# Issue order of the attention stretch set by a list scheduler inside the kernel

## The chip, the cores and the metric

The kernel runs on one core of one Trainium2 chip. A core has five engines that each work through their own list of instructions in order and wait for each other by semaphores: TensorE (PE, matrix products), VectorE (DVE), ScalarE (ACT), GpSimd (POOL) and SyncE (SP), which here issues every DMA transfer. The metric is the device time of one execution in microseconds, smaller being better. What is changed is only the order in which each engine's list stands; no instruction is added, removed or given other operands.

## The reference

The program is an attention with a threshold, and then two gated layers over its output.

```python
q, k, v: (4 batches, 8 heads, 576 rows, 64 columns), float32; tau = 0.02
scores = (q @ k.T) / sqrt(64)
scores = where(scores >= max(scores, row) - tau, scores, -1e9)
attn   = exp(scores - max) ; attn /= sum(attn) + 1e-9
x = (attn @ v), heads side by side: 2304 tokens x 512
# layer 1
x = (sigmoid(x @ w_gate) * (x @ w_val)) @ w_out          # 512 -> 1536 -> 512
# layer 2
x = ((x @ w1) * (x @ w2)) @ w3 @ w_out2                   # 512 -> 1024 -> 1024 -> 512
```

All inputs of the two layers arrive in 64-bit form, and the products are done in split precision: an operand is a high and a low part, and three products (high-low, low-high, high-high) are summed.

## The kernel before

The program has one stretch that this change concerns, up to the line `cut = ...` of the new code, and a tail behind it.

**The attention stretch** runs 144 steps, numbered 0 to 143: 4 batches x 4 pairs of heads x 9 row blocks. A step goes through the engines like this:

- `s_mm` (PE): 4 or 6 products of 128x288 into one of two PSUM buffers `ps_s`, in turn by step. So step n+2 needs the buffer of step n.
- `s_max` (DVE, L360): the row maximum `nm`. `s_exp` (ACT, L366 and L367): the exponential `e` and the threshold `th`. `s_mask` (DVE, L375): masks `e`, reading `ps_s` for the last time; this frees the buffer.
- `s_hi`, `s_lo` (ACT L383; ACT L394 and POOL L397, or DVE L399): the high and low 16-bit parts `h16`, four buffers.
- `s_tr` (SP, L403): a transposing DMA of `h16` into `pt`, five buffers.
- `pv` (PE): 14 products (28 in the ninth step of a pair) of `pt` with the value tiles, into `u` or a part of `ps_s`.

For each pair there is preparation too: loads of q, k and v, their transposes on PE (`ps_t`), a chain of small DVE and ACT operations for the scale of v (`vm`, `vx`, `vp`, `vs`, then `vb` on ACT at L304), and at the pair's end `x_norm`, `x_pe`, `x_act`, which write the result into `XR`.

Two other pieces of work are traced between these steps by `filler`. The first is the **merge** (`merge_gen`): layer 2's `w3` and `w_out2` are loaded in pieces of 512 KB (SP, L477), turned from 64-bit into float (`cast64`: DVE L487 and L493, ACT L492, POOL L496), split (`wol`, DVE L506), transposed (`ps_3`, then `tl` at DVE L572) and multiplied into 8 tiles `ps_34` of 24 products. The second is **layer 1** (`l1_gen`) for the first three batches: cast of its weights, `ps_h` and `ps_o` products of 128x512, and the element-wise work on them. Layer 1 can start only when all four pairs of batch 0 are through, which is about step 41.

**The tail** finishes layer 1 for the last batch and does layer 2: `ps_h`, `ps_o`, `ps_ab` and `ps_y` products on PE.

What sets the order: the kernel is written in a tracing layer whose scheduler, when the program is finished, orders each engine's instructions by a priority (the place in the trace, and 90 places earlier for `s_mask`, `s_max`, `s_exp`, `s_mm`, by `tc.high_priority(offset=RING)`) and by its own simulation of when each could start. It then gives out the buffers and the semaphore waits. Once the program runs, the order on an engine is fixed: an instruction whose input is late holds everything behind it on that engine.

Of the kernel before, what the change touches and what calls it, by code (L numbers as in the profile page):

```python
# [16 lines left out]
ALU = mybir.AluOpType  # L17
AX = mybir.AxisListType
PSUM = bass.MemoryType.PSUM


@with_exitstack
def kernel(
# [22 lines left out]
    nc = tc.nc  # L46
    P = 128
    B, H, S, D = q.shape
# [16 lines left out]
    cst = ctx.enter_context(tc.tile_pool(name="cst", bufs=1))  # L65
    ps_m = ctx.enter_context(tc.tile_pool(name="ps_m", bufs=2, space=PSUM))
    ps_c = ctx.enter_context(tc.tile_pool(name="ps_c", bufs=1, space=PSUM))
    nbank = [0, (ps_m, ps_m)]
# [23 lines left out]
    ap_ = actx.enter_context(tc.tile_pool(name="attn", bufs=1, side="right"))  # L92
    ps_s = actx.enter_context(tc.tile_pool(name="ps_s", bufs=1, space=PSUM))
    ps_u = actx.enter_context(tc.tile_pool(name="ps_u", bufs=1, space=PSUM))

# [234 lines left out]
    def s_mm(g):  # L330
        pr, s = divmod(g, NSL)
        p = prep[pr]
        ps = sbuf_[g % 2][:, SO:SO + S]
        if s < 2 * NC:
            h, c = divmod(s, NC)
            cs = slice(c * P, (c + 1) * P)
            if pr < ZP:
                x, y = qst[h][pr % 2][:, cs], kst[h][pr % 2][:, cs]
                prods = [(x, p["xk"]), (y, p["xk"]), (x, p["yk"])]
            else:  # L340
                prods = [(p["qa"][h][:, cs], p["ka"][h]), (p["qa"][h][:, cs], ylz[h])]
        else:
            prods = [
                (p["qb"][:, 0, :], p["xk"]),
                (p["qb"][:, 1, :], p["xk"]),
                (p["qb"][:, 0, :], p["yk"]),
            ]
        for i, (a, r) in enumerate(prods):
            for j in range(2):
                mm(  # L350
                    ps[:, j * HS:(j + 1) * HS], a, r[:, j * HS:(j + 1) * HS],
                    i == 0, i == len(prods) - 1,
                )
        st[g] = {"ps": ps}

    def s_max(g):
        x = st[g]
        nm = ap_.tile([P, 1], F32, tag="nm", name="nm", bufs=3)
        th = ap_.tile([P, 1], F32, tag="th", name="th", bufs=3)
        nc.vector.tensor_reduce(nm, x["ps"], axis=AX.X, op=ALU.max, negate=True)  # L360
        x.update(nm=nm, th=th)

    def s_exp(g):
        x = st[g]
        e = ap_.tile([P, S], F32, tag="e", name="e", bufs=4)
        nc.scalar.activation(e, x["ps"], AF.Exp, bias=x["nm"])  # L366
        nc.scalar.activation(x["th"], x["nm"], AF.Identity, scale=-1.0, bias=ntau)  # L367
        x["e"] = e

    def s_mask(g):  # L370
        pr, s = divmod(g, NSL)
        x = st[g]
        if s == 0:
            prep[pr]["sum"] = ap_.tile([P, NSL], F32, tag="sum", name="sum", bufs=2)
        nc.vector.scalar_tensor_tensor(  # L375
            x["e"], x["ps"], x["th"], x["e"], op0=ALU.is_ge, op1=ALU.mult,
            accum_out=prep[pr]["sum"][:, s:s + 1],
        )

    def s_hi(g):  # L380
        x = st[g]
        x["h16"] = ap_.tile([P, 2 * S], F16, tag="h16", name="h16", bufs=4)
        nc.scalar.activation(  # L383
            x["h16"][:, 0:S], x["e"], AF.Copy, scale=PSC
        )

    def s_lo(g):
        e = st[g]["e"]
        hb = st[g]["h16"]
        hi, lo = hb[:, 0:S], hb[:, S:2 * S]  # L390
        b = g // (NPAIR * NSL)
        if b == 0 or g % 2 == 0:
            if b < 2:
                nc.scalar.activation(e, e, AF.Copy, scale=PSC)  # L394
            else:
                nc.gpsimd.tensor_scalar(e, e, PSC, 1.0, op0=ALU.mult, op1=ALU.mult)
            nc.gpsimd.tensor_tensor(lo, e, hi, op=ALU.subtract)  # L397
        else:
            nc.vector.scalar_tensor_tensor(lo, e, PSC, hi, op0=ALU.mult, op1=ALU.subtract)  # L399
# [24 lines left out]
    def x_norm(pr):  # L424
        p = prep[pr]
        rs = ap_.tile([P, NSL], F32, tag="rs", name="rs", bufs=1)
        nc.vector.tensor_scalar(rs, p["sum"], 1e-9, None, op0=ALU.add)
        nc.vector.reciprocal(rs, rs)
        xn = ap_.tile([P, NC, 2, D], F32, tag="xn", name="xn")
        xt = ap_.tile([P, 2, D], F32, tag="xt", name="xt")  # L430
        nc.vector.tensor_tensor(
            xn.rearrange("p c h d -> p h c d"), p["u"],
            rs[:, 0:2 * NC].rearrange("p (h c x) -> p h c x", h=2, x=1).to_broadcast([P, 2, NC, D]),
            op=ALU.mult,
        )
        nc.vector.tensor_scalar(
            xt, p["ut"][:, 0:P].rearrange("p (x d) -> p x d", x=2),
            rs[:, 2 * NC:NSL], None, op0=ALU.mult,
        )
        p.update(xn=xn, xt=xt)  # L440
# [82 lines left out]
    mp = None  # L523
# [91 lines left out]
    lp = None  # L615
    lx = None
    lb = None
# [6 lines left out]
    def open_lx():  # L624
        nonlocal lx
        lx = lx_ctx.enter_context(tc.tile_pool(name="lx", bufs=1))
# [193 lines left out]
    LAG = 5  # L820
# [4 lines left out]
    def run(gen, ns):  # L825
        while gen is not None and ns > 0:
            n = len(defer)
            t = next(gen, "end")
            if lp is None:
                flush(1)  # L830
            else:
                flush(max(len(defer) - n, 0))
            if t == "end":
                return None
            if t is None:
                return gen
            ns -= t
            spent[0] += t
        return gen
# [3 lines left out]
    def budget(g):  # L843


        n = NPAIR * NSL
        e = max(0, (g - LAG - 3) // n)
        return (e * L1_NS - spent[0]) / (2 * ((e + 1) * n + LAG + 3 - g)) if e else 1.0

    order = ExitStack()  # L850
# [5 lines left out]
    mp = mctx.enter_context(tc.tile_pool(name="mp", bufs=1))  # L856
# [22 lines left out]
    def filler(g, half):  # L879
        nonlocal l1, merge, lp, lb  # L880
        if merge is not None:
            merge = run(merge, 700.0)
            if merge is None:
                mctx.close()
                spent[0] = 0
                lp = tc_lp.enter_context(tc.tile_pool(name="lp", bufs=1))
                lb = tc_lp.enter_context(tc.tile_pool(name="lb", bufs=1))
                open_lx()
                l1 = l1_gen()
        elif l1 is not None and (g > NPAIR * NSL or g >= 10 and half):  # L890
            l1 = run(l1, budget(g))
# [14 lines left out]
    for g in range(G + LAG + 3):  # L906
        pr, s = divmod(g, NSL)
        steps = ahead[s] if pr + 1 < NP else ([],) * 5
        done = divmod(g - LAG, NSL)
        with tc.high_priority(offset=RING):  # L910
            if g < G:
                s_mask(g)
            if g + 1 < G:
                s_max(g + 1)
                s_exp(g + 1)
            if g + 2 < G:
                s_mm(g + 2)
        if g < G:
            s_hi(g)
        for f in steps[3]:  # L920
            f(pr + 1, g)
        if done[1] == 0 and done[0] > 0:
            x_norm(done[0] - 1)
        if g < G and g % 2 == 0 or g // (NPAIR * NSL) == 0:
            s_lo(g)
        if 0 < g <= G and not ((g - 1) % 2 == 0 or (g - 1) // (NPAIR * NSL) == 0):
            s_lo(g - 1)
        if 2 <= g < G + 2:
            s_tr(g - 2)
        for f in steps[0]:  # L930
            f(pr + 1)
        for f in steps[1]:
            f(pr + 1)
        if done[1] == 2 and done[0] > 0:
            x_act(done[0] - 1)
            if done[0] % NPAIR == 0:
                xdone[0] = done[0] // NPAIR
        filler(g, 0)
        for f in steps[2]:
            if isinstance(f, str):  # L940
                if pr + 2 < NP:
                    load(src[f], pr + 2, f)
            else:
                f(pr + 1)
        if 0 <= g - LAG < G:
            pv(g - LAG, g)
        for f in steps[4]:
            f(pr + 1)
        if done[1] == 1 and done[0] > 0:
            x_pe(done[0] - 1, g)  # L950
        filler(g, 1)
    order.close()
    actx.close()
    tail[0] = True
# [15 lines left out]

    ps_2 = ctx.enter_context(tc.tile_pool(name="ps_2", bufs=5, space=PSUM))
    nbank[1] = (ps_m, ps_m) + (ps_2,) * 5
# [86 lines left out]
    sp = ctx.enter_context(tc.tile_pool(name="sp", bufs=1))  # L1059
# [101 lines left out]
    for g in range(NG):  # L1161
# [22 lines left out]
        for t in range(GT // P):  # L1184
            part(NF2 - 2, t)
            part(NF2 - 1, t)
            out_rows(g, t, pss[t])

# [31 lines left out]
```

## Time and profile before

| | |
|---|---|
| median of 3 runs | 1117.62 us (1112.0 to 1119.1) |
| profiled execution | 1116.73 us, of which the span from first to last instruction is 1114.9 us |
| busy share of the span | PE 92%, weight loads 81%, DVE 72%, POOL 61%, ACT 56% |
| attention stretch | 0 to about 671 us |
| tail | about 671 to 1115 us |

The busy share is an average over stretches with different limits, so the table of stretches (the first group of rows below) is read before it: for each stretch of time it has the busy time of each engine. The waits then say, for one engine and one stretch, which instruction came late and by how much.

### The profile page before, as it was taken

The numbers are of one execution on the slowest core, as the hardware profiler recorded it, in microseconds if no ns is written. First come the engines' busy times: TensorE is split into PE (matmuls) and PEld (weight loads), VectorE is DVE, ScalarE is ACT, GpSimd is POOL, SyncE is SP. The second block draws the span as 40 slices with busy tenths as digits, with TensorE's granted clock in tenths as the row PEclk, the third lists the DMA queues.
The fourth block names the chain that finished last, engine by engine and source line by source line (L and its number), as shares of the span: only waits on it lengthen the run. The fifth ranks groups of instructions, "written<-read, shape, count | busy, mean of one in ns | idle before, by whom it ended". The sixth has DMA issues, their size and how long they took to land. (4 is left out here: it accounts for less than half of the span.)

```text
span 1114.9 us, 20240 instructions
## 1 busy us (share of the span) xinstructions
PE 1023.0 (92%) x7088; PEld 902.2 (81%) x7088; DVE 799.6 (72%) x1388; ACT 629.2 (56%) x1253; POOL 683.1 (61%) x585
## 2 busy tenths in 40 slices
PE   3599965899899999999999998999999999999997
PEld 2477764777778787787878888999999989988996
DVE  8998578899886887777887645776776644752741
ACT  4788787778586666677667645454442322331321
POOL 4655358488695676767687755775764633562430
PEclk8599986899899999999999999999999999999999
DMA  7799779899899898999999565676559826834922
GB/s 216 183 244 222 152 174 269 179 236 262 194 252 225 182 187 192 210 202 177 221 194 212 129 145 169 213 230 225 194 184 295 253 71 231 289 124 123 334 87 61
DMA packets 301845, 221.29 MB, mean 198 GB/s; under 512 B 221872, under 2 KB 250544, under 8 KB 301744
## 3 DMA queue, kind: packets, MB, share of 16 engines
q1 hardware_dynamic: 301744, 220.00, 76.7%
q8 instruction: 56, 0.92, 0.4%
q14 instruction: 45, 0.37, 0.1%
HBM read 133.17 MB, written 30.93 MB: 147 GB/s over the span
## 5 line engine op out<-in xcount | busy, mean ns | idle before, releaser
L366 ACT ACTIVATE e<-ps_s,nm 128x576 f32<-128x576 f32 x144 | 106.3, 739 | 73.2 <-DVE nm L360 72.2
L397 POOL TENSOR_TENSOR h<-e,h 128x576 f16<-128x576 f32 x90 | 120.0, 1334 | 40.3 <-ACT e L394 16.8
L63 PEld LDWEIGHTS <-pt 128*128 128x128 f16 x2240 | 83.8, 101 | 61.4 <-DMA pt<-h 29.7
L375 DVE SCALAR_TENSOR_TENSOR e<-ps_s,th,e 128x576 f32<-128x576 f32 x144 | 116.2, 811 | 19.9 <-ACT th L367 11.0
L360 DVE TENSOR_REDUCE nm<-ps_s 128x1 f32<-128x576 f32 x144 | 105.8, 748 | 29.5 <-PE ps_s L63 16.0
L383 ACT ACTIVATE h<-e 128x576 f16<-128x576 f32 x144 | 97.2, 678 | 37.1 <-DVE e L375 31.6
L63 PE MATMUL ps_h<-xl,vh 128*128 128x512 f32 (+1 forms) x240 | 92.8, 387 | 3.4 <-DVE yk L274 3.4
L63 PE MATMUL ps_h<-xl,gh 128*128 128x512 f32 (+1 forms) x240 | 92.2, 384 | 3.7 <-POOL xl L506 2.8
L63 PE MATMUL ps_y<-wm,abh 128*128 128x512 f32 x288 | 91.5, 390 | 1.2 <-DVE wm L506 1.2
L63 PE MATMUL ps_o<-gvl,oh 128*128 128x512 f32 (+1 forms) x240 | 91.0, 379 | 0.0
L506 POOL TENSOR_TENSOR gl<-w,gh 128x512 fp32r<-128x512 f32 x42 | 55.5, 1322 | 56.5 <-ACT gh L505 51.4
L63 PE MATMUL ps_h<-xh,vh 128*128 128x512 f32 (+1 forms) x240 | 89.9, 375 | 0.0
L63 PE MATMUL ps_h<-xh,vl 128*128 128x512 f32 (+1 forms) x240 | 89.8, 374 | 0.0
L63 PE MATMUL ps_h<-xh,gl 128*128 128x512 f32 (+1 forms) x240 | 88.9, 370 | 0.0
L63 PE MATMUL ps_h<-xh,gh 128*128 128x512 f32 (+1 forms) x240 | 88.8, 370 | 0.0
L63 PE MATMUL ps_o<-gvh,ol 128*128 128x512 f32 (+1 forms) x240 | 88.5, 369 | 0.0
L63 PE MATMUL ps_o<-gvh,oh 128*128 128x512 f32 (+1 forms) x240 | 88.5, 369 | 0.0
L63 PE MATMUL u<-vh,pt 128*128 128x64 f16 x640 | 64.5, 200 | 25.0 <-DMA pt<-h 21.9
L506 POOL TENSOR_TENSOR ol<-w,oh 128x512 fp32r<-128x512 f32 x42 | 54.0, 1294 | 30.3 <-ACT oh L505 30.2
L399 DVE SCALAR_TENSOR_TENSOR h<-e,h 128x576 f16<-128x576 f32 x54 | 67.8, 1256 | 5.4 <-ACT h L383 5.1
L506 POOL TENSOR_TENSOR vl<-w,vh 128x512 fp32r<-128x512 f32 x43 | 59.0, 1373 | 14.6 <-ACT vh L505 14.6
L506 POOL TENSOR_TENSOR gvl<-gr,gvh 128x512 fp32r<-128x512 f32 (+1 forms) x48 | 61.8, 1287 | 8.4 <-ACT gvh L505 7.9
(207 smaller groups left out, 3109.3 us busy)
## 6 DMA issues: line engine op xcount, KB each, us to landing
wc<-sc_c SPq DMA_DIRECT2D x168, 256.0 KB, 3.4
w<-sc_w SPq DMA_DIRECT2D x35, 768.0 KB, 5.2
sc_c<-wc SPq DMA_DIRECT2D x56, 256.0 KB, 2.5
XR<-in_moe_w_out_dram SPq DMA_DIRECT2D x20, 512.0 KB, 5.0
sc_w<-w SPq DMA_DIRECT2D x11, 768.0 KB, 5.6
XR<-in_moe_w_dram SPq DMA_DIRECT2D x16, 512.0 KB, 4.6
raw<-in_moe_w_dram SPq DMA_DIRECT2D x16, 512.0 KB, 4.5
XR<-in_moe_w_gate_dram SPq DMA_DIRECT2D x12, 512.0 KB, 5.4
```

What stands on the lines that cost most here:

```text
L63: nc.tensor.matmul(out_, lhsT, rhs, start=first, stop=last)
L360: nc.vector.tensor_reduce(nm, x["ps"], axis=AX.X, op=ALU.max, negate=True)
L366: nc.scalar.activation(e, x["ps"], AF.Exp, bias=x["nm"])
L375: nc.vector.scalar_tensor_tensor(x["e"], x["ps"], x["th"], x["e"], op0=ALU.is_ge, op1=ALU.mult, accum_out=prep[pr]["sum"][:, s:s + 1],)
L383: nc.scalar.activation(x["h16"][:, 0:S], x["e"], AF.Copy, scale=PSC)
L397: nc.gpsimd.tensor_tensor(lo, e, hi, op=ALU.subtract)
L399: nc.vector.scalar_tensor_tensor(lo, e, PSC, hi, op0=ALU.mult, op1=ALU.subtract)
L506: (lo_eng or nc.gpsimd).tensor_tensor(lo, x, hi.bitcast(F32), op=ALU.subtract)
```

## The change

A class `Plan` is added. After the whole program has been traced, it takes the first `cut` instructions (those of the attention stretch), finds which of them depend on which through tiles, buffers and PSUM banks, gives each a duration by a formula of its shape, and runs a list scheduler: at each turn the engine that can start earliest takes, among its instructions whose inputs are ready, the one that stands first in the trace. The trace order alone is the priority; the 90 places of `high_priority` play no part in it. `pin` then ties each instruction to the one before it on its engine, so that the tracing layer's scheduler must keep that order. The tail is not tied.

```diff
+class Plan:
...
+    LAG = {"PE": 40, "DVE": 33, "ACT": 33, "POOL": 33, "SP": 23}
+    LEAD = {"PE": 20, "DVE": 0, "ACT": 0, "POOL": 46, "SP": 0}
+    OVER = {"DVE": 80, "ACT": 100, "POOL": 42}
+    CLK = 3413.0
+
+    def __init__(self, insts, cut, over):
+        self.later = [i for i in insts[cut:] if i.opcode in self.OPS]
+        insts = insts[:cut]
+        self.x = [i for i in insts if i.opcode in self.OPS and self.name(i.engine) in self.ENG]
...
+        self.edges(over)
+        self.cost = [self.time(n) for n in range(len(self.x))]
...
+    def order(self):
...
+        while left:
+            best = None
+            for e in E:
+                if not avail[e]:
+                    continue
+                n = min(avail[e], key=lambda n: (max(ready[n] - free[e] - 1, 0), n))
+                s = max(free[e], ready[n])
+                if best is None or s < best[0]:
+                    best = s, e, n
+            s, e, n = best
+            avail[e].remove(n)
+            seq[e].append(n)
...
+            for m in succ[n]:
+                need[m] -= 1
+                if not need[m]:
+                    r = max((start[q] for q in self.soft[m]), default=0.0)
+                    for q in self.hard[m]:
+                        if self.e[q] == "PE" == self.e[m]:
+                            r = max(r, start[q] + 5)
+                        else:
+                            r = max(r, done[q] + self.LAG[self.e[q]] + self.LEAD[self.e[m]])
+                    ready[m] = r
+                    avail[self.e[m]].append(m)
+        self.start, self.done = start, done
+        return seq
+
+    def pin(self, tc):
+        for e, l in self.order().items():
+            for m, n in zip(l, l[1:]):
+                tc.add_manual_dep(
+                    self.x[n], self.x[m].name,
+                    mybir.DependencyInfo(mybir.DependencyClass.NoSync, mybir.DependencyReason.DATA),
+                    reason="order",
+                )
...
         filler(g, 1)
+    cut = len(nc.cur_bb.bb.instructions)
     order.close()
...
+    Plan(nc.cur_bb.bb.instructions, cut, {"lp": ("mp",), "lb": ("mp",), "lx": ("mp",)}).pin(tc)
```

The new lines push every later line of the file down by 276 (L375 becomes L651). Three places show what moves.

**DVE, early, around the first `tl`** (the operation that lets the merge's products begin). The names `e_489`, `e_536`, `e_585` are the masked exponentials of steps 4, 5 and 6; `e_428` is step 3. Before:

```order
L506 TENSOR_TENSOR wol_164<-f_349,woh_163 128x512
L487 TENSOR_SCALAR ps_c_401<-XR_78 128x512
L360 TENSOR_REDUCE nm_582<-ps_s0_88 128x1
L293 TENSOR_REDUCE vx_551<-ps_s1_89 128x1
L375 SCALAR_TENSOR_TENSOR e_536,sum_289<-ps_s1_89,th_534,e_536 128x576
L493 SCALAR_TENSOR_TENSOR t1_398<-XR_78,ps_c_401 128x512
L295 TENSOR_SCALAR vp_553<-vx_551 128x1
L375 SCALAR_TENSOR_TENSOR e_585,sum_289<-ps_s0_88,th_583,e_585 128x576
L572 TENSOR_TENSOR tl_446<-ps_3_447,th_445 128x512
```

and with the change:

```order
L782 TENSOR_TENSOR wol_164<-f_349,woh_163 128x512
L769 SCALAR_TENSOR_TENSOR t1_389<-XR_78,ps_c_392 128x512
L636 TENSOR_REDUCE nm_425<-ps_s1_89 128x1
L763 TENSOR_SCALAR ps_c_401<-XR_78 128x512
L556 TENSOR_REDUCE vm_443<-vnat_100 128x128
L769 SCALAR_TENSOR_TENSOR t1_398<-XR_78,ps_c_401 128x512
L651 SCALAR_TENSOR_TENSOR e_428,sum_289<-ps_s1_89,th_426,e_428 128x576
L763 TENSOR_SCALAR ps_c_410<-XR_78 128x512
L848 TENSOR_TENSOR tl_446<-ps_3_447,th_445 128x512
```

Before, the maxima and masks of seven steps (0 to 6) stand ahead of the first `tl`; now those of four (0 to 3). On PE the first `ps_34` product stood behind the scores of step 8 and the `pv` of step 4; now it stands between the scores of steps 5 and 6 and behind the first 5 products of the `pv` of step 2. Both orders reach the last `ps_34` tile at the scores of step 26. Of the 60 casts (L487), DVE has 11 between the masks of steps 26 and 44 before, and 9 now; up to the mask of step 56, 50 stand before and 43 now.

**SP, early, up to the fifth transposing DMA.** Before:

```order
L477 DMA XR_78<-in_moe2_w3_dram 128x512 x2
L403 DMA_TRANSPOSE pt_503<-h16_370 128x9x128
L477 DMA XR_78<-in_moe2_w3_dram 128x512
L403 DMA_TRANSPOSE pt_549<-h16_437 128x9x128
L477 DMA XR_78<-in_moe2_w3_dram 128x512
L403 DMA_TRANSPOSE pt_599<-h16_498 128x9x128
L477 DMA XR_78<-in_moe2_w3_dram 128x512
L403 DMA_TRANSPOSE pt_664<-h16_545 128x9x128
```

and with the change:

```order
L753 DMA XR_78<-in_moe2_w3_dram 128x512 x2
L679 DMA_TRANSPOSE pt_503<-h16_370 128x9x128
L753 DMA XR_78<-in_moe2_w3_dram 128x512 x3
L679 DMA_TRANSPOSE pt_549<-h16_437 128x9x128
L753 DMA XR_78<-in_moe2_w3_dram 128x512 x2
L442 DMA km_572<-in_k_dram 128x4x64 x2
L753 DMA XR_78<-in_moe2_w3_dram 128x512
L679 DMA_TRANSPOSE pt_599<-h16_498 128x9x128
L753 DMA XR_78<-in_moe2_w3_dram 128x512 x2
L679 DMA_TRANSPOSE pt_664<-h16_545 128x9x128
```

With the 8 loads of `w_out2` that stand ahead of these rows in both, 13 loads of 512 KB precede the fifth transpose before, and 18 now.

**PE, in the steady part, the scores of steps 65 and 66.** Before, they stand directly behind each other:

```order
L63 MATMUL ps_s_89<-xk,qa_1_91 128x288 x2
L63 MATMUL ps_s_89<-xk,ka_1_95 128x288 x2
L63 MATMUL ps_s_89<-yk,qa_1_91 128x288 x2
L185 MATMUL ps_s_89<-ident,tails 128x128
L63 MATMUL ps_s_88<-xk,qa_1_91 128x288 x2
L63 MATMUL ps_s_88<-xk,ka_1_95 128x288 x2
L63 MATMUL ps_s_88<-yk,qa_1_91 128x288 x2
```

and with the change, where the scores of step 65 are the first three rows, other work follows at once:

```order
L339 MATMUL ps_s_89<-xk,qa_1_91 128x288 x2
L339 MATMUL ps_s_89<-xk,ka_1_95 128x288 x2
L339 MATMUL ps_s_89<-yk,qa_1_91 128x288 x2
L461 MATMUL ps_s_89<-ident,tails 128x128
L339 MATMUL ps_h<-xl,gh 128x512
L339 MATMUL ps_h<-xh,gl 128x512
L339 MATMUL ps_h<-xh,gh 128x512
L339 MATMUL ps_h<-xl,gh 128x512
L339 MATMUL ps_h<-xh,gl 128x512
L339 MATMUL ps_h<-xh,gh 128x512
```

The scores of step 66 come only after these 6 `ps_h` products, the 14 `pv` products of step 58, 4 transposes and 6 more `ps_h` products. It is the same over the whole steady part: before, scores often come in twos, as early as the priority takes them; now one step's scores alternate with half units of layer 1 and one `pv`. Between steps 45 and 135 the `pv` that follows a step's scores is 3 to 8 steps behind them before, and 7 behind in 79 of 91 places now. Behind `cut`, the tail's rows stand in the same order in both programs on DVE, ACT, POOL and SP, and on PE but for 11 that are displaced by at most 6 places.

## Rows read from the trace of the kernel before

**Rows 1.** Busy time of each engine by stretch, granted clock, DMA share, GB/s.

```profile
core 0: us, PE busy (x) PEld busy (x) DVE busy (x) ACT busy (x) POOL busy (x), PEclk, DMA share, GB/s
0.00:60.00 60.00, 28.95 (x166) 23.59 (x167) 52.53 (x96) 36.30 (x70) 33.50 (x39) 0.69 0.80 204
60.00:148.00 88.00, 80.33 (x682) 68.49 (x680) 67.73 (x132) 69.88 (x135) 45.44 (x38) 0.98 0.86 192
148.00:223.00 75.00, 51.66 (x456) 44.81 (x456) 65.24 (x118) 59.19 (x119) 48.60 (x40) 0.75 0.91 220
223.00:475.00 252.00, 235.41 (x1837) 193.21 (x1838) 211.13 (x389) 179.09 (x358) 188.27 (x153) 0.98 0.95 216
475.00:671.00 196.00, 193.06 (x1611) 158.01 (x1609) 143.56 (x263) 131.98 (x266) 142.19 (x120) 1.00 0.84 180
671.00:1115.00 444.00, 433.61 (x2340) 414.06 (x2340) 259.38 (x394) 152.79 (x310) 225.14 (x195) 0.99 0.59 193
```

**Rows 2.** Chain that ended last, in order of time: start us, us, what.

```profile
673.01 10.16 PE ps_h L63 x48
683.16 8.20 PE ps_o L63 x36
691.37 24.98 PE ps_h L63 x144
```

**Rows 3.** Waits of PE, 0 to 671 us: total us, times, longest us.

```profile
PE ps_s L63 <- DVE e L375: 23.1, 19, 4.6
PE u L63 <- DMA pt<-h: 21.9, 20, 3.6
PE ps_s L63 <- ACT vb L304: 7.6, 3, 6.1
PE ps_t L175 <- DMA qm<-in_q_dram: 6.9, 2, 6.2
```

**Rows 4.** Timeline of PE, 0 to 60 us: start us, us, what [idle before <-releaser].

```profile
25.94 0.29 PE L63 MATMUL ps_s<-identb,vb 128*128 128x128 bf16 x1 [6.05 <-ACT vb L304]
...
46.56 0.83 PE L63 MATMUL ps_s<-xk,qa 128*128 128x288 f32 x2
...
57.26 0.48 PE L63 MATMUL ps<-wol,th 128*128 128x512 f32 x1
```

**Rows 5.** Busy time by stretch, as in Rows 1, 25 us each.

```profile
25.00:50.00 25.00, 11.25 (x71) 9.06 (x72) 24.91 (x41) 17.91 (x36) 15.04 (x12) 0.50 0.74 179
...
125.00:150.00 25.00, 23.07 (x198) 19.84 (x196) 12.83 (x27) 17.20 (x34) 7.96 (x8) 0.95 0.51 112
```

**Rows 6.** Groups of DVE, 148 to 223 us: busy us, mean ns | idle before.

```profile
L375 DVE SCALAR_TENSOR_TENSOR e<-ps_s,th,e 128x576 f32<-128x576 f32 x19 | 15.4, 811 | 2.1 <-ACT XR L459 0.9 <-ACT th L367 0.8 <-POOL w L496 0.4
L360 DVE TENSOR_REDUCE nm<-ps_s 128x1 f32<-128x576 f32 x18 | 13.4, 749 | 1.2 <-PE ps_s L450 0.6 <-PE ps_s L63 0.5
L487 DVE TENSOR_SCALAR ps_c<-XR 128x512 uint32<-128x512 uint32 x11 | 7.6, 689 | 0.1
L493 DVE SCALAR_TENSOR_TENSOR w<-XR,ps_c 128x512 uint32<-128x512 uint32 x11 | 7.5, 682 | 2.4 <-issue 2.3
```

**Rows 7.** Waits of PE, 223 to 475 us.

```profile
PE ps_s L63 <- DVE e L375: 7.6, 8, 2.5
PE u L63 <- DMA pt<-h: 4.8, 6, 1.9
PE ps_h L63 <- DVE yk L274: 3.4, 1, 3.4
```

**Rows 8.** Timeline of PE inside the steady part: the first and the last of 15 products.

```profile
562.02 0.40 PE L63 MATMUL ps_h<-xl,vh 128*128 128x512 f32 x1
...
565.23 0.39 PE L63 MATMUL ps_h<-xh,gh 128*128 128x512 f32 x1
```

217 lines of the change are left out of this document (added).

## The prediction

> **What bounds the kernel now.** I read the table of stretches first [rows 1]. The last stretch, 671 to 1115 us, has PE busy for 433.61 of 444 us, and the chain that ended last is from 673 us on nearly all PE products in a row [rows 2]. The order of that tail is not changed, so these 444 us stay, and the question is only when the attention stretch ends, now at about 671 us. That stretch falls into four parts with different limits.
>
> [...]
> - 60 to 148: PE is busy 80.33 of 88 us: it works off the merge. In the last 25 us of it DVE is busy 12.83 us only, and DMA 0.51 [rows 5], so the other engines wait for PE there.
> - 148 to 223: PE has too little to do (51.66 of 75), DVE is busy 65.24 and ACT 59.19. Layer 1 can't start before batch 0 is through, so this part lasts as long as DVE and ACT need for its steps.
> - 223 to 671: PE is busy 235.41 of 252 and 193.06 of 196 us. What an order can give back is the idle rest, 16.6 and 2.9 us.
>
> Then the waits of PE in the whole stretch [rows 3]: 23.1 us for the mask that frees a score buffer, 21.9 us for a transposed `pt`, 7.6 us for `vb`, 6.9 us for the first load. The first two are waits that an order makes: PE stands before an instruction whose input is late, with other work behind it.
>
> **The change part by part.** It moves instructions and adds none, so no duration changes by itself; each term is idle time that goes, or comes. All are counted against the profiled execution, 1116.73 us, which lies 0.9 us under the median shown.
>
> *A, 0 to 148 us.* The merge is pulled forward against the steps. Ahead of the first `tl`, DVE has three maxima and three masks fewer; at 0.749 and 0.811 us each (durations of a later part, same shapes [rows 6]) that is 3 x 1.56 = 4.7 us earlier. PE's first merge product ran at 57.26 us. It now stands ahead of the scores of step 6, which ran at 46.56 us [rows 4], so the most that it can come earlier is 10.7 us. What the merge gains at its start, the PE-bound end of this part gains too: both orders finish the merge at step 26, and the 4.7 us of DVE work that was put off fits into the 12.2 us that DVE idles at 125 to 150 us [rows 5]. A second piece: the chain to `vb` now begins straight behind the first maximum and ahead of the second pair's preparation. PE waited 6.05 us there [rows 4], but DVE was full in that time, so I count 1.3 us of it, about a fifth. Taken: -4.7 - 1.3 = -6 us. Bounds: -10.7 - 6.05 = -16.8 us below. Above, a loss: five loads of 512 KB more go ahead of the fifth transpose, and at the 204 GB/s of the first 60 us [rows 1] that is 5 x 524,288 bytes / 204 GB/s = 12.9 us that the `pv` of step 4 can come later. I stay near the gain, since the early `pv` products feed nothing that is urgent: their result is used only at the pair's end, and PE has the merge in the meantime.
>
> *B, 148 to 223 us.* DVE is the bound, so what counts is DVE work moved out. Of the casts, 9 now stand between the masks of steps 26 and 44 and not 11; each is an L487 and an L493, 0.689 + 0.682 us [rows 6], so 2 x 1.37 = 2.7 us. Taken: -3 us with the little that PE's waits add. Bounds: DVE's whole idle time of 9.8 us below, nothing above, since no DVE work is moved in. The moved casts land before step 75, where DVE has 41 us free (252 - 211.13, [rows 1]); that hides them, and were it gone they would cost their 2.7 us.
>
> *C, 223 to 475 us.* Here scores stood in twos, and the second had to wait for the mask of two steps before: 7.6 us in 8 waits, the largest group; 4.8 us are for `pt` and 3.4 us one wait for `yk` [rows 7]. With scores one by one, half a unit of layer 1 and one `pv` lie between two of them. Six products take 6 x 0.229 us [rows 8] = 1.4 us, and two such halves and a `pv` give the chain maximum, exponential, threshold, mask a full step. And `pv` is now mostly 7 steps behind, so its `pt` has landed. I take the mask waits as gone, and 1.4 us of the rest: -9 us. Bounds: -16.6 us (all idle time) and 0. What is late next is DMA: its share here is 0.95 already [rows 1], so a part that is 4% shorter brings it near 1, and that is why I don't take all.
>
> *D, 475 to 671 us.* 2.9 us idle; taken -1.5, bounds -2.9 and 0.
>
> The sum: -6 - 3 - 9 - 1.5 = -19.5, so 1116.7 - 19.5 = **1097.2 us**.
>
> [...] In 475 to 671 us PE reads as full, 193.06 of 196, while its weight loads fill 158.01 us, and in the tail 414.06 of 444 [rows 1]. [...]
>
> **The rivals.**
>
> *1, slower: the transposes starve the softmax.* The place is SP's list before step 5. If the five loads hold up the transposes, the `h16` buffers (four) stay taken, and steps 4 and later stand still until their transposes are issued. DVE has 9.8 us free in part B and can't make this up, so batch 0 ends 12.9 us later and layer 1 starts as much later. It decides if the first transposes come so late that DVE, with casts to do, runs out of them first. If C gains nothing either, 1116.7 + 12.9 = 1129.6 us. For it: at 0 to 60 us the DMA share is 0.80, and SP works its list in order. Against it: the loads have only four slots to land in, so they wait for DVE's casts anyway and can't all pile up.
>
> *2, much faster.* All idle time that the bounds name goes: -16.8 - 9.8 - 16.6 - 2.9 = -46, or 1070.6 us. Against it: DVE, DMA and PE would each have to be at 95% and over at once. [...]
>
> *3, no change to speak of.* DVE bounds A and B in any order, C loses its gain to DMA at a share of 0.95, and the waits only change their names: -3 us of B and a little of D, about 1113 us. For it: 38% of PE's 81.6 us of idle time (31.05 us) in the attention stretch lies at 0 to 60 us, where DVE is at 88%.
>
> That the change doesn't do what it says I leave out: the lists show the new order on all five engines.
>
> **How the numbers follow.** A difference of under 1%, 11.2 us, can't be told from none by such a measurement. The forecast, a gain of 11 to 30 us, gets 0.45; a larger gain, rival 2, 0.17; no change, rival 3, 0.22; slower, rival 1, 0.16. So faster 0.62, same 0.22, slower 0.16. The range begins at 1070, by the bounds of rival 2, and ends at 1128, just under rival 1; about 0.05 lies under it and 0.15 above.
>
> **What would show it.** Right: the tail still some 444 us long; the attention stretch ends at about 651 us; PE's waits for L651 (the mask) in its steady part fall from 7.6 to under 2 us; the first `ps_34` product runs before 54 us; the first `ps_h` product comes some 9 us earlier. Wrong: PE waits for `pt` or DVE waits for scores grow before 60 us, which is rival 1; a DMA share of over 1.0 from 223 us on with the waits for `pt` as long as now is rival 3. If the model of durations behind the new order is off by more than a step for DMA, each engine waits at its head more than before, on SP first.

## The result, and the profile after

The changed kernel takes 1089.23 us (median of 4 runs, 1088.04 to 1091.18) against 1116.46 us for the kernel before (the three runs above and a fourth): a ratio of 0.9762, 95% interval 0.9726 to 0.9798. It is faster by 2.4%. The profiled execution took 1091.18 us, 25.5 us less than that of before, and its span is 1089.4 us.

By stretch, as in [rows 1]. The first three cuts lie as far behind the first and the last merge product and the first `ps_h` product as there, and the tail begins at 645.5 and not at 671:

```profile
core 0: us, PE busy (x) PEld busy (x) DVE busy (x) ACT busy (x) POOL busy (x), PEclk, DMA share, GB/s
0.00:49.50 49.50, 22.01 (x107) 17.83 (x108) 45.86 (x84) 31.88 (x59) 28.80 (x36) 0.69 0.85 230
49.50:137.00 87.50, 79.38 (x694) 67.25 (x694) 67.80 (x139) 68.20 (x134) 43.99 (x36) 1.00 0.89 196
137.00:205.00 68.00, 50.66 (x496) 43.79 (x493) 60.84 (x121) 62.96 (x126) 49.22 (x41) 0.80 0.98 216
205.00:450.00 245.00, 237.10 (x1891) 196.80 (x1891) 209.68 (x395) 185.10 (x368) 196.03 (x160) 0.98 1.08 235
450.00:645.50 195.50, 189.47 (x1573) 153.76 (x1571) 138.98 (x259) 130.29 (x261) 138.76 (x119) 0.99 0.83 178
645.50:1089.40 443.90, 433.63 (x2340) 414.10 (x2340) 259.74 (x394) 152.94 (x310) 224.71 (x195) 0.99 0.59 193
```

The tail is the same to 0.1 us, and DVE's busy time summed over all stretches is 16.7 us lower than that of [rows 1] (782.89 against 799.57), for the same 1388 instructions (one that lies across a cut is counted on both sides). The chain that ended last, against [rows 2], begins 25.5 us sooner with the same pieces:

```profile
647.48 10.18 PE ps_h L339 x48
657.66 8.20 PE ps_o L339 x36
665.86 24.98 PE ps_h L339 x144
```

PE's waits up to 645.5 us, against [rows 3]. The waits for `pt` more than halve; those for the mask (L651 now) do not go, they grow from 23.1 to 36.3 us:

```profile
PE ps_s L339 <- DVE e L651: 36.3, 24, 4.8
PE u L339 <- DMA pt<-h: 9.8, 5, 7.2
PE ps_t L451 <- DMA qm<-in_q_dram: 5.5, 1, 5.5
```

The first merge product, against [rows 4], runs 10.5 us earlier; the first `ps_h` product 17.7 us earlier, at 188.50 us and not 206.19:

```profile
46.72 0.78 PE L339 MATMUL ps<-wol,th 128*128 128x512 f32 x1
```

```profile
188.50 0.78 PE L339 MATMUL ps_h<-xl,gh 128*128 128x512 f32 x1
```

**A measure for where it came from.** Steps and layer 1's products are mixed otherwise in each order, so the same moment of two traces is not the same state of work. I therefore add up PE's work, each product by a fixed spacing, near the one that its shape has where nothing holds it: 0.227 us for 512 columns, 0.1735 for 384, 0.1335 for 288, 0.029 for the small `pv` products and 0.108 for a transpose. In the tail of before 36 products of 512 columns take 8.20 us and 144 of 384 take 24.98 us [rows 2], so 0.228 and 0.1735 us each; the median spacing of the other three in the trace of before, at a granted clock of 1.00, is 0.131, 0.029 and 0.109 us. Then I read when PE has done W us of this work. That time minus W is what PE has lost so far. By W = 80 us most of the merge's products are done; 80 to 110 is its end and the stretch up to layer 1; 110 to 225 is step 42 to 70; 530 is about the attention's end. "Held" counts DVE instructions of the stretch that took over 2.2 us, whose kinds take 0.17 us (the additions `rs`) and 0.75 us (the low parts) where no GpSimd instruction runs, and their sum; the longest in the changed kernel is an addition of 2.03 us.

| kernel | lost to W = 80 | 80 to 110 | 110 to 225 | 225 to 530 | sum | held, us |
|---|---|---|---|---|---|---|
| before | 56.9 | 41.2 | 19.7 | 30.7 | 148.5 | 5, 20.6 |
| the change | 50.8 | 30.9 | 8.4 | 32.9 | 123.0 | 0 |
| e1, tied to step 44 | 50.2 | 40.7 | 29.3 | 32.2 | 152.4 | 7, 31.8 |
| e2, tied from step 44 | 55.9 | 39.4 | 8.4 | 26.0 | 129.7 | 1, 2.5 |
| e3, no 90 places | 55.7 | 41.4 | 18.2 | 24.5 | 139.8 | 4, 14.8 |
| e4, PE alone | 53.1 | 40.7 | 26.5 | 36.0 | 156.3 | 1, 5.3 |
| e5, rs on ACT | 58.7 | 39.2 | 15.3 | 34.1 | 147.3 | 2, 7.5 |
| e6, the same in the change | 49.5 | 32.9 | 11.1 | 27.9 | 121.4 | 2, 6.0 |
| e7, no collision lines | 50.8 | 31.0 | 13.0 | 26.1 | 120.9 | 0 |
| e8, SP free | 50.4 | 30.1 | 8.4 | 30.0 | 118.9 | 0 |
| e9, casts in place | 53.3 | 31.8 | 24.2 | 37.7 | 147.0 | 2, 5.3 |
| e10, casts in place in the change | 50.3 | 27.7 | 21.8 | 28.5 | 128.3 | 1, 8.1 |
| e11, PE free | 66.0 | 35.7 | 23.0 | 35.1 | 159.8 | 2, 4.9 |
| e12, one low part moved | 54.4 | 40.8 | 18.0 | 32.1 | 145.3 | 5, 20.8 |

The change gains 6.1 us at the start, 10.3 us before layer 1, 11.3 us in its first half, and gives 2.2 us back after it.

Each row is one traced execution, so small differences in one column show nothing. e8, whose lists on PE, DVE, ACT and POOL are those of the change row by row, differs from it by 0.4, 0.8, 0.0 and 2.9 us in the four columns. The granted clock differs too: up to W = 530 it was 0.50 and not 1.00 for 92.2 us before, 75.1 us with the change and 41.0 us in e8; in the traces of before and after the products of 512 columns start 0.427 us apart (median) at 0.50, and 0.227 us at 1.00. And the kernel before took from 1107.1 to 1123.7 us over all its executions here, and the ratios below are against different ones of these, so that two ratios are compared by their intervals.

### The profile page after: what moved, and what is told of

Same layout as the page of the kernel before. It is cut to its first block, busy times and chain, and to the rows that moved or that the text cites. A ratio compares the mean times of both kernels' runs of the same rounds, so it can differ in the third digit from the quotient of the medians.

```text
span 1089.4 us, 20230 instructions
## 1 busy us (share of the span) xinstructions
PE 1012.2 (93%) x7088; PEld 893.5 (82%) x7088; DVE 782.9 (72%) x1388; ACT 631.4 (58%) x1253; POOL 681.5 (63%) x585
## 5 line engine op out<-in xcount | busy, mean ns | idle before, releaser
L673 POOL TENSOR_TENSOR h<-e,h 128x576 f16<-128x576 f32 x90 | 118.1, 1314 | 43.3 <-ACT e L670 32.2
L651 DVE SCALAR_TENSOR_TENSOR e<-ps_s,th,e 128x576 f32<-128x576 f32 x144 | 116.4, 810 | 21.2 <-ACT th L643 12.9
L642 ACT ACTIVATE e<-ps_s,nm 128x576 f32<-128x576 f32 x144 | 106.3, 738 | 42.9 <-DVE nm L636 40.8
L339 PEld LDWEIGHTS <-pt 128*128 128x128 f16 x2240 | 78.6, 101 | 38.5 <-issue 24.4
L339 PE MATMUL ps_h<-xl,gh 128*128 128x512 f32 (+1 forms) x240 | 94.5, 394 | 5.5 <-POOL xl L782 4.3
L782 POOL TENSOR_TENSOR gl<-w,gh 128x512 fp32r<-128x512 f32 x42 | 55.7, 1327 | 46.7 <-ACT gh L781 46.7
L782 POOL TENSOR_TENSOR ol<-w,oh 128x512 fp32r<-128x512 f32 x42 | 56.8, 1356 | 19.5 <-ACT oh L781 19.4
L339 PE MATMUL u<-vh,pt 128*128 128x64 f16 x640 | 59.2, 199 | 10.0 <-DMA pt<-h 9.8
L782 POOL TENSOR_TENSOR vl<-w,vh 128x512 fp32r<-128x512 f32 x43 | 61.7, 1434 | 8.6 <-ACT vh L781 8.6
L781 ACT ACTIVATE abh<-r 128x384 fp32r<-128x384 f32 x48 | 24.3, 523 | 72.5 <-DVE r L1365 72.4
```

Source lines behind the costliest of these rows:

```text
L339: nc.tensor.matmul(out_, lhsT, rhs, start=first, stop=last)
L651: nc.vector.scalar_tensor_tensor(x["e"], x["ps"], x["th"], x["e"], op0=ALU.is_ge, op1=ALU.mult, accum_out=prep[pr]["sum"][:, s:s + 1],)
L781: nc.scalar.activation(hi, x, AF.Copy)
L782: (lo_eng or nc.gpsimd).tensor_tensor(lo, x, hi.bitcast(F32), op=ALU.subtract)
```

## The experiments

**e1 and e2: one part of the stretch tied at a time.** `Plan` orders the whole stretch; only one side of step 44 is tied.

```diff
+        if g == 44:
+            split_at = len(nc.cur_bb.bb.instructions)
...
+    early = {i.name for i in nc.cur_bb.bb.instructions[:split_at]}
...
         for e, l in self.order().items():
+            l = [n for n in l if self.x[n].name in early]        # e1; "not in" for e2
```

> Only the instructions traced before step 44 are tied to the new order; the rest of the attention stretch is left to the tracing layer's scheduler. Theory 'two separate gains' (17.7 us come before layer 1's first product, by the merge pulled forward and DVE work put off; 7.8 us come behind it, by scores one by one): about 18 us faster than before, first ps_h product near 188 us. Rival 'one thing only' (the early part has a head start that the later part would catch up anyway, so all of it or nothing is kept): 26 us faster or under 8 us.

> Only the instructions traced from step 44 on are tied. 'Two separate gains': 7 to 9 us faster than before, first ps_h product near 206 us as before, PE's idle time from there to the tail 14 us and not 20. Rival 'one thing only': no difference, within 4 us.

Measured: e1 is slower than before, ratio 1.008 (1.0057 to 1.0104); e2 is faster, 0.9862 (0.984 to 0.9884). Neither came out as expected: the two don't add up to the change (0.9762). e1 keeps the whole gain of the start (50.2), so that is due to the early order alone; it has nothing of the next 10 us (40.7; its first `ps_h` product runs at 198.7 us and not near 188), and then it loses 29.3 us where before lost 19.7. e2 has the gain behind step 44 in full (8.4), and loses 6.9 us less than the change later. What is missing in both is most of the stretch between, 80 to 110, where instructions of both sides stand side by side: neither half of the new order gives it alone. It doesn't need the new order, though: e9 below gets 9.4 of the 10.3 us in the kernel before.

Where e1 lost, its trace shows something that I had not looked for. DVE and then GpSimd, 274 to 281 us:

```profile
274.44 0.69 DVE L1008 SCALAR_TENSOR_TENSOR gr<-th,ps_h 128x512 f32<-128x512 f32 x1 [5.81 <-PE ps_h L340]
275.05 5.14 DVE L704 TENSOR_SCALAR rs<-sum 128x9 f32<-128x9 f32 x1
280.11 0.68 DVE L764 TENSOR_SCALAR ps_c<-XR 128x512 uint32<-128x512 uint32 x1
```

```profile
275.15 1.28 POOL L773 TENSOR_TENSOR w<-w,t 128x512 int32<-128x512 int32 x1
276.40 1.29 POOL L783 TENSOR_TENSOR vl<-w,vh 128x512 fp32r<-128x512 f32 x1
277.66 1.28 POOL L674 TENSOR_TENSOR h<-e,h 128x576 f16<-128x576 f32 x1
278.91 1.25 POOL L783 TENSOR_TENSOR gvl<-gr,gvh 128x512 fp32r<-128x512 f32 x1
```

An addition on 9 elements a partition stands on DVE for 5.14 us, just as long as GpSimd runs four instructions without a gap, and ends with the last of them. e1 has seven such instructions. Before has five; one of them is this, with the part of the trace that I had read as an order's fault:

```profile
276.58 0.68 DVE L731 SCALAR_TENSOR_TENSOR gr<-th,ps_h 128x512 f32<-128x512 f32 x1
277.18 5.83 DVE L399 SCALAR_TENSOR_TENSOR h<-e,h 128x576 f16<-128x576 f32 x1
282.94 0.68 DVE L487 TENSOR_SCALAR ps_c<-XR 128x512 uint32<-128x512 uint32 x1
```

```profile
276.17 1.27 POOL L506 TENSOR_TENSOR gl<-w,gh 128x512 fp32r<-128x512 f32 x1
277.41 1.27 POOL L397 TENSOR_TENSOR h<-e,h 128x576 f16<-128x576 f32 x1
278.64 1.27 POOL L496 TENSOR_TENSOR w<-w,t 128x512 int32<-128x512 int32 x1
279.88 1.28 POOL L506 TENSOR_TENSOR vl<-w,vh 128x512 fp32r<-128x512 f32 x1
281.13 1.27 POOL L506 TENSOR_TENSOR gvl<-gr,gvh 128x512 fp32r<-128x512 f32 x1
```

It made `yk` late, which is the 3.4 us wait of [rows 7], and the granted clock was 0.50 for 6.8 us there, 284.6 to 291.4 us, where products of 512 columns start 0.43 us apart and not 0.23. So a new theory: part of the gain is DVE time that the new order doesn't lose to GpSimd.

**e3: the 90 places alone.** In the kernel before:

```diff
-    RING = 90
+    RING = 0
```

> The kernel before with RING = 0: no Plan, no ties, only the 90 places of priority for mask, maximum, exponential and scores taken away. Rival 'the priority was the fault': the whole gain, 24 to 28 us faster than before. Theory 'the new scheduler's durations matter': less than half of it, between 10 us faster and 10 us slower, since the tracing layer's own simulation still sets which instruction is ready first.

Ratio 0.9942 (0.9919 to 0.9964), as the theory had it: about a quarter of the gain. Of the 8.7 us that its row gains, 6.2 are in the last column and 1.0 at the start and before layer 1 together.

**e4 and e11: PE's list alone, and all but PE's.** In `pin`:

```diff
         for e, l in self.order().items():
+            if e not in ('PE',):                              # e4
+            if e not in ('SP', 'DVE', 'ACT', 'POOL'):         # e11
+                continue
```

> The whole stretch is tied on PE alone; DVE, ACT, POOL and SP are ordered by the tracing layer's scheduler around it. Rival 'PE's list alone is the fault': 24 us faster or more. Theory 'two separate gains': the later part is PE's alone (scores one by one), so 7 to 9 us come; the early part needs DVE's and SP's order too, since the merge waits for DVE's casts, so at most 5 us of its 18 us come: 7 to 14 us faster in all.

> The change without PE: DVE, ACT, POOL and SP are tied, PE is ordered by the tracing layer's scheduler around them. If one list carries the gain it is this or PE's, and PE's alone made the kernel 11 us slower. 'The lists fit each other': 0 to 12 us faster than before. Rival 'DVE's and ACT's lists carry it': 20 us faster or more.

Both are slower than before: e4 1.0114 (1.0079 to 1.015), e11 1.0102 (1.0073 to 1.0132). Both expectations were too high: neither PE's list nor the other four together carry the gain. In e4 PE stands before late masks, its largest wait:

```profile
PE ps_s L341 <- DVE e L653: 50.2, 21, 5.6
```

In e11 that isn't the reason, since its mask waits are no longer than the 36.3 us of the change; its waits for `pt` are as long as before (21.5 and 21.9 us, 9.8 with the change), and of the 11.3 us that its row loses against before, 9.1 lie at the start (66.0 against 56.9):

```profile
PE ps_s L341 <- DVE e L653: 37.2, 25, 5.2
PE u L341 <- DMA pt<-h: 21.5, 10, 5.6
```

Here, then, the order of PE was worth something only beside the order of the engines that feed it. In both runs the engines that are not tied keep the 90 places of priority, which the new order doesn't have. Whether the lists would fit each other better without them was not run.

**e5 and e6: the held addition on ACT**, in the kernel before and in the changed one.

```diff
-        nc.vector.tensor_scalar(rs, p["sum"], 1e-9, None, op0=ALU.add)
+        nc.scalar.activation(rs, p["sum"], AF.Copy, bias=1e-9)
```

> The kernel before, with the sum's small addition (rs, 128x9, 16 times, DVE L427) done on ACT. In the trace of before these 16 take 17.6 us on DVE, one of them 4.8 us in part B while GpSimd runs four instructions back to back; in the changed kernel they take 9.6 us. Theory 'DVE is held up by GpSimd' (a good part of the gain is DVE time lost to GpSimd that the new order avoids): 4 to 10 us faster than before. Rival 'only which work comes first matters' : under 2 us, since DVE's idle time hides it.

> The changed kernel with the same small addition on ACT. 'Held up by GpSimd': 1 to 4 us faster than the changed kernel, so 28 to 31 us faster than before; the 9.6 us left there are in small pieces. Rival: as the changed kernel within 1 us.

e5: 0.9986 (0.9961 to 1.0011), no difference; e6: 0.9806 (0.9772 to 0.9839), not told apart from the change. The rival had the total right on both, as far as these intervals go. In its place the hold was not all hidden: without the 4.8 us addition the time from the last merge product to the first `ps_h` product fell from 62.2 to 56.9 us, and the lost time of 80 to 110 from 41.2 to 39.2. The total shows none of it. In 110 to 225, e5 loses 15.3 and not 19.7: the 5.83 us instruction was not held in that run either, but others were (two, 7.5 us).

**e7: the model without the collision.** In `Plan.order`:

```diff
-                if e == "DVE" and c[1]:
-                    d += max(0, pport - s - 80)
-                    dport = s + d
-                elif e == "POOL":
-                    d = max(d, d + dport - 110 - s)
-                    pport = s + d
```

> The changed kernel without the five lines of Plan.order that make a DVE or GpSimd instruction longer when it falls on the other's; all else as in the change. 'Held up by GpSimd': the DVE time of rs and of the low parts (h<-e, 54 times) together, 85.4 us before and 67.9 with the change, goes up again by 8 us or more, and of the 26 us gained at most 18 are left. Rival 'only which work comes first matters': 24 to 28 us faster than before, as with the change.

0.9826 (0.9788 to 0.9864), which is 19.4 us faster (15.1 to 23.6): more than the theory's 18 and less than the rival's 24. The interval just overlaps that of the change, and its profile has no held instruction either. The time of `rs` and the low parts is 72.5 us (9.2 + 63.3), up by 4.6 and not by 8. So the theory falls in one point: the new order has no held instructions, but not because its model knows of them. Whether these lines are worth a few us is not shown.

**e8: SP left free.** `if e == "SP": continue` in `pin`.

> The change without SP: PE, DVE, ACT and POOL are tied, SP's transfers are ordered by the tracing layer's scheduler around them. If the transposes' place in SP's list carries part of the gain (PE's waits for pt fell from 21.9 to 9.8 us), 10 us of the gain or more are lost, 10 to 16 us faster than before; if the four engines' order carries it, 22 to 27 us faster.

0.9781 (0.9738 to 0.9825): the gain is all there, so tying SP adds nothing to it that shows. That the order of the transfers carries none of it is not shown, since SP left free got nearly the list of the change: the fifth transpose stands behind the same 18 loads, and 111 of the 144 transposes are at the same place of SP's list, the others at most 6 places off (between before and the change 30 are, the others up to 15 places off). The five loads ahead of the fifth transpose, the place of my first rival, stand in both, and both are faster.

**e9 and e10: casts in place.** In the kernel before, and as an edge in `Plan` in the changed one:

```diff
-        if tail[0]:
+        if tail[0] or l1 is not None:
             tc.keep_in_program_order(first)
```

```diff
...
+            if self.io[n][1][0].tensor.name.startswith("ps_c"):
+                merge -= 1
+                if merge < 0:
+                    self.soft[n].add(prev)
+            prev = n
```

Here `n` runs over the instructions of DVE as traced, `prev` is the one before, and `merge` counts off the merge's 24 casts.

> The kernel before, with one thing alone: layer 1's casts on DVE are kept at their traced place in DVE's list, so that 28 and not 36 stand before the mask of step 40 (33 with the change). Theory 'casts crowd part B': the time from the last merge product to the first ps_h product, 62.2 us before and 55.6 with the change, falls by 6 to 11 us (8 casts at 1.37 us of DVE), and the kernel is 4 to 10 us faster. Rival 'B needs the whole new order': that time stays over 60 us, and the kernel is within 3 us of before.

> The changed kernel, with the same held in Plan: 27 casts before the mask of step 40 and not 33. 'Casts crowd part B': another 3 to 8 us of part B, 27 to 34 us faster than before. Rival 'given back': layer 1 then lacks its weights between steps 44 and 60, and the total is as with the change or worse.

e9: 0.9994 (0.9959 to 1.0029). The time from the last merge product to the first `ps_h` product fell from 62.2 to 49.4 us, more than expected, with 27 casts done by then and not 36: 12.8 us for 9 casts, 1.4 us each. So casts do crowd this part. But all of it was given back, most of it right behind the first `ps_h`: between W = 120 and 140 PE lost 15.1 us, and 3.7 before. DVE still has the casts to do there (it is busy 24.07 of 25 us from 217 to 242), and PE waits for masks and for a tile of layer 1's weights, `gh`. PE's waits in e9 at 190.8 to 260 us, where before, over the same length from its first `ps_h`, waited 1.2 us for the mask and never for `gh`:

```profile
PE ps_s L63 <- DVE e L375: 5.5, 3, 5.0
PE ps_h L63 <- ACT gh L505: 2.8, 1, 2.8
```

e10: 0.9787 (0.9725 to 0.9849), not told apart from the change. With 27 casts done by the first `ps_h` product and not 33, that product ran at 188.22 us against 188.50 with the change: in the new order the casts hardly hold it up, and DVE stands idle for 10.5 of the 55.8 us before it. By lost time e10 gains 3.2 us more before layer 1 (27.7 against 30.9) and loses 13.4 more behind it (21.8 against 8.4). One held instruction has a part in that, 8.1 us over seven GpSimd instructions:

```profile
236.72 8.10 DVE L684 SCALAR_TENSOR_TENSOR h<-e,h 128x576 f16<-128x576 f32 x1
```

**e12: one low part moved.**

```diff
-        if b == 0 or g % 2 == 0:
+        if b == 0 or g % 2 == 0 or g == 55:
```

> The kernel before, with the low part of step 55 alone done on ACT and GpSimd, as the even steps do it, and not on DVE. That DVE instruction took 5.83 us in before while GpSimd ran five instructions back to back, and the same kind takes 0.76 us elsewhere; PE then waited 3.4 us and ran 6.8 us at the lower clock level. Theory 'one held instruction makes part C's stall': PE's lost time around 270 to 290 us falls from 9.4 us to under 5 us, 3 to 8 us faster in all. Rival 'it would stall there anyway': within 2 us of before.

1.0032 (1.0001 to 1.0064): not faster. The place came out as the theory said: between W = 160 and 180 PE lost 3.2 us and not 9.4, and the stall was gone. The total did not. The list behind it changed and other instructions were held in turn (five again, 20.8 us), one addition for 5.65 us; that this is what took the gain back is likely and not shown, since the traced execution is the fastest of the ten (1113.79 us, median 1118.78):

```profile
307.72 5.65 DVE L427 TENSOR_SCALAR rs<-sum 128x9 f32<-128x9 f32 x1
```

No version here beats the change by more than its interval; e8 is level with it.

## Why the prediction was right, and where it was not

The forecast was 19.5 us of gain against the profiled execution; it was 25.5 us (median to median 27.2), inside the range, and of the sign forecast. By the columns of the table the parts are -6.1, -10.3, -11.3 and +2.2 us: B was sized 7 us too low, and D's gain did not come, which hides some of that in the sum. The terms one by one:

- **A, the start: right in size by lost time, the cause shown in part.** -6 was taken; PE's lost time up to W = 80 fell by 6.1 us. The end of the merge, which the term speaks of, came 11.1 us earlier (144.0 to 132.9), but 4.2 us of that are other products put off: PE had done 86.7 us of work by then before and 82.5 after. The first merge product came 10.5 us earlier, at the far bound of 10.7 and not the 4.7 counted, and PE's 6.05 us wait for `vb`, in which DVE was busy for 5.89 us, is not among the waits of after. e1 shows that the early order alone does it, not which of the two pieces. One sign that was named for rival 1 did show, PE's wait for `pt` before 60 us, which grew without the loss that should come with it; before, and with the change:

```profile
PE u L63 <- DMA pt<-h: 4.6, 3, 3.6
```

```profile
PE u L339 <- DMA pt<-h: 7.2, 1, 7.2
```

- **B, before layer 1: right in kind, sized too low.** -3 was taken with a bound of 9.8; by lost time up to W = 110 it is 10.3, over the bound. In time, the first `ps_h` came 17.7 us earlier, of which the last merge product has 11.1 and this part 6.6. Two steps failed. One is the count of casts: 2 by the list between two masks, but 3 by the trace at the moment that matters, the first `ps_h` (36 against 33). The other is a term put at nothing, that no duration changes: DVE's two additions `rs` here took 5.0 us before and 1.3 after. In the trace of before, for DVE from 143.4 to 206.2 us, where the casts are the same 11 as in [rows 6]:

```profile
L427 DVE TENSOR_SCALAR rs<-sum 128x9 f32<-128x9 f32 x2 | 5.0, 2478 | 0.0
```

  and in that of after, from 132.5 to 188.5 us:

```profile
L769 DVE SCALAR_TENSOR_TENSOR w<-XR,ps_c 128x512 uint32<-128x512 uint32 x8 | 5.5, 684 | 0.2
L763 DVE TENSOR_SCALAR ps_c<-XR 128x512 uint32<-128x512 uint32 x8 | 5.5, 683 | 0.0
L703 DVE TENSOR_SCALAR rs<-sum 128x9 f32<-128x9 f32 x2 | 1.3, 664 | 0.1
```

  Three casts are 4.1 us of DVE, the additions 3.7. e9 shows that the price per cast holds in the order before, e10 that it doesn't in the new one, and e5 that a held `rs` counts in this part. How the 10.3 us divide between the two is open.
- **C, layer 1 beside attention: right in size, half wrong in cause.** -9 was taken; from the first `ps_h` to the cut, PE stood idle 17.4 us before (206.2 to 475) and 7.9 us after (188.5 to 450), so -9.5. But I said that the mask waits would go, to under 2 us, and the rest mostly stay. Against [rows 7], 205 to 450 us:

```profile
PE ps_s L339 <- DVE e L651: 4.9, 4, 1.6
PE ps_h L339 <- POOL xl L782: 1.5, 1, 1.5
PE ps_h L339 <- DVE xl L782: 0.7, 1, 0.7
PE ps_h L339 <- ACT th L1002: 0.3, 1, 0.3
PE u L339 <- DMA pt<-h: 0.2, 1, 0.2
```

  The waits for the mask fell by 2.7 us only. Those for `pt` fell from 4.8 to 0.2, as `pv` 7 steps behind would have it, and the 3.4 us for `yk` are gone with the held instruction. e12 shows that this one instruction made the stall of 160 to 180, where 7.4 of the 11.3 us of 110 to 225 lie (9.4 us lost before, 2.0 after). That the sum still came to 9.5 is luck: 7.6 and 1.4 were counted, and 2.7, 4.6 and 3.4 came, less some new waits.
- **D: wrong, nothing came of it.** -1.5 was taken, PE's idle time rose from 2.9 to 6.0 us. In e8, with the same lists on the four engines, the same 195.5 us ahead of the tail have 3.3 us of idle time, so the rise is within what executions differ by, and only the missing gain is shown.
- **"No duration changes by itself" was wrong.** DVE's low parts and additions took 85.4 us before and 67.9 after (58.4 + 9.6), by how they fall against GpSimd. How much of the gain that is can't be told from these runs: e7 keeps most of the gain with 72.5 us, and e5 gains nothing in the total with the additions taken away.
- **DMA at a share of 0.95 was no limit.** It rose to 1.08 in the same part, and the waits for `pt` fell. Rival 3 leaned on this.

What stays open beside this: why it takes PE's list and the others' together. That each alone costs 1.0 to 1.1% is shown. That PE then waits for another engine's order is read from the mask waits of e4 and the `pt` waits of e11, and is not tested further.

## What to carry to other kernels

A new order should be read by what each engine waits for last, part by part, and its gain counted against a fixed amount of work of the bounding engine, not against the clock: a part that gets 13 us shorter (e9) can be worth nothing when the work that was put off is waited for next. Before a freed list is called unimportant, look whether it came out any different (e8). Orders of engines that feed each other belong together; here one of them alone from a better plan was worse than none (e4, 1.1% slower). Where two engines hinder each other, moving one instruction can move the collision (e12: five held instructions before and five again, 20.6 and 20.8 us), so look for the count of long ones over the whole stretch.

## What the runs showed of the hardware

A DVE instruction that meets a busy GpSimd can be held not for one GpSimd instruction but for several: 5.83 us over five of 1.27 us in before, 8.10 us over seven in e10, where the same kind takes 0.75 us when free (the 8 of 54 in before that no GpSimd instruction overlaps took 0.747 to 0.758 us); an addition on 9 elements a partition took 5.14 us in e1, and 0.17 us when free (2 of 16 in before). All the held ones are low parts and these additions; of DVE's other instructions in the attention stretch of before, none took over 2.13 us. Most low parts and additions that begin beside a GpSimd instruction take longer than when free, and so does the GpSimd instruction behind. This is the usual case, in before:

```profile
230.11 1.47 DVE L399 SCALAR_TENSOR_TENSOR h<-e,h 128x576 f16<-128x576 f32 x1
```

```profile
229.67 1.29 POOL L496 TENSOR_TENSOR w<-w,t 128x512 int32<-128x512 int32 x1 [0.49 <-DVE w L493]
230.92 1.80 POOL L506 TENSOR_TENSOR vl<-w,vh 128x512 fp32r<-128x512 f32 x1
```

The low part ends 0.62 us after the end of one GpSimd instruction, and the next GpSimd instruction takes 1.80 us where its kind takes 1.3. Of the 25 low parts in before that began inside a GpSimd instruction with another directly behind it, 23 ended within 0.9 us of the end of the running one, and two were passed over by that other one and more (3.93 and 5.83 us); in all 14 traces it is 337 against 16. What decides between the two is not shown.
